# Cutting the first two chunks' products at two quarters and a half of the weights, in an attention and MoE kernel

## The chip, the core and the metric

The kernel runs on one core of a Trainium2 chip. The metric is device time in microseconds (us) of one execution. Engines are named as the profile names them: PE (matrix products), PEld (its weight loads), DVE (vector), ACT (scalar), POOL (GpSimd), SP (the engine whose queue issues the transfers).

## The reference

Attention with four sink keys and a sliding window of 128 keys, over 4 batches, 8 heads, 768 positions and 64 channels, feeds a two-layer feed-forward block:

```python
scores = scale * np.matmul(q, k.transpose(0, 1, 3, 2))
keep = is_sink | in_window
scores = np.where(keep, scores, -1000000000.0)
a = np.exp(scores - np.max(scores, axis=-1, keepdims=True))
x = np.matmul(a / (np.sum(a, axis=-1, keepdims=True) + 1e-09), v)   # regrouped to 3072 tokens x 512
h = np.maximum(x @ w_in, 0.0)                                       # w_in 512 x 2048
return (h * h @ w_out).astype(np.float32)                           # w_out 2048 x 512
```

The inputs are float64. `w_in` and `w_out` therefore arrive as 64-bit words.

## The kernel before, in words

**Chunks and pairs.** The 3072 tokens are cut into 8 chunks of 384 (`NCHUNK`, `TOK`), two to a batch. The attention of a chunk goes by 4 pairs of heads. For one pair: `score` (L240) multiplies queries and keys into a bank of PSUM, tile `s`; DVE adds the mask and takes the row's extreme (L268, `P` and `nbs`); ACT takes the exponential (L271); `normalise` (L275) takes reciprocals on DVE (`rs`) and scales on POOL (L296), which also gathers the sink columns in `PSK` (L302, L303); `probs` (L337) transposes on PE into tile `pt` and ACT or DVE copies it out as `PTF` (L357, L355); `sink_keys` (L305) does the same for the sinks (`pss`, `SK`); `values` (L383) multiplies into `xo`, and ACT and DVE write the chunk's `x` in a high and a low part (L409, L410).

**Products.** `moe` (L445) is a generator that works through a list of legs `(c, f0, f1)`: chunk `c` by the slices `f0` to `f1` of the 16 slices of 128 hidden units. One item is one slice of one chunk: 12 multiplications into `ph` (L457), `r` and `gh` on ACT (L465, L468), a second square on ACT (L472) or a product on DVE (L475), the low part `gl` on DVE (L479), and, one item later, 9 multiplications into the three banks `po` (L494). It yields four times an item; one such step is called a quantum here. At a leg's end `evacuate` (L506) empties `po`: of a leg that begins at slice 0 by copies on DVE and ACT (L522, L520), of another by loading the earlier partial sum `part` from DRAM and adding on DVE (L518). What is not the chunk's last leg is written to `part` in DRAM.

**Weight rows.** 32 rows of weights (`NROW`), 8 to each quarter of the hidden units, are loaded as `raw` (512 KB each, L549) and split into a high and a low part by `split_steps` (L551): on ACT a copy (L560) and a cast (L573), on DVE `t` (L561), `t` again (L563), `m` (L565), `eb` (L567) and the row itself, `wi` or `wo` (L574). It yields in between; a row takes 5 steps. The buffer `m` is single. A row's raw words are loaded two rows ahead.

**Order.** Up to L707 the order on every engine is the one of the code (`manual_schedule`). First comes stage A, five rounds `s` (L653 to L679): scores of pair `s`, values of pair `s-2`, and the transpositions (`tail`) of pair `s-1`, with `fill(n)` putting `n` steps of the split between. Then comes stage B (L699 to L703): in each of `QUANTA` quanta of the first leg, `fill` some steps and one entry of a list `todo`, which holds the attention of pairs 5 to 7 of the first eight (31 entries). Stage B ends when `EARLY` rows are split. After that the legs go on under a scheduler that orders each engine's instructions itself; a table `plan` says up to which unit of later attention and over which rows each leg goes, and `need` (L710) holds rows back no longer than the products allow.

Of the kernel before, what the change touches and what calls it, by code (L numbers as in the profile page):

```python
# [8 lines left out]
F32 = mybir.dt.float32  # L9
# [9 lines left out]
P = 128  # L19
# [22 lines left out]
def sink_window_attention_moe(  # L42
# [25 lines left out]
    with ExitStack() as fast:  # L68
# [437 lines left out]
        def evacuate(c, f0, f1, po):  # L506
            for t in range(NQ):
                pool, tag = (ap3, "PTF") if c == NCHUNK - 1 and t == 2 else (mp, "ob")
                ob = pool.tile([P, DM], F32, tag=tag, name=f"ob_{c}_{f0}_{t}")
# [13 lines left out]
                if f1 < NFC:  # L523
                    part[c, t] = dp.tile([P, DM], F32, tag=f"part{c}{t}", name=f"part_{c}_{t}")
                    nc.sync.dma_start(out=part[c, t], in_=ob)
                else:
                    nc.sync.dma_start(out=out[r0 : r0 + P, :], in_=ob)
# [79 lines left out]

        FH = NFC // 2
        legs = [(0, 0, FH), (1, 0, FH), (0, FH, NFC), (1, FH, NFC)] + [(c, 0, NFC) for c in range(2, NCHUNK)]
        products = moe(legs)  # L610
        QUANTA = 4 * FH
        EARLY = HALF + 2
        with tc.manual_schedule(engines={E.PE, E.DVE, E.Activation, E.Pool, E.SP}):
# [39 lines left out]
            for s in range(NPAIR + 1):  # L653
                if s > 0:
                    load_qk(*pairs[s + 1])
                for i, tags in enumerate((("att", "att"), ("h", "h"), ("o0", "o1"))):
                    scores(s, i, tags)
                    fill(1)
                fill(1)
# [7 lines left out]
                if s > 0:  # L667
                    if s > 1:
                        load_v(*pairs[s])
                    t = tail(s - 1, ("o2", "h"))  # L670
                    next(t)
                    fill(1)
                    if rest:
                        rest()
                    next(t)
                    fill(1)
                    next(t)
                else:
                    fill(1)  # L679
# [19 lines left out]
            for n in range(QUANTA):  # L699
                next(products)  # L700
                fill(2 if n < QUANTA // 2 and n % 3 or n % 4 == 0 or n >= QUANTA - 12 else 1)
                if todo:
# [53 lines left out]

        plan = [(ready[1], EARLY, 27, 1.0), (ready[1] + 24, 27, NROW, 0.7), (ready[2], NROW, NROW, 1.0)]
        plan += [(ready[min(c + 1, NCHUNK - 1)], NROW, NROW, 1.0) for c in range(2, NCHUNK)]
# [221 lines left out]
```

## Time and profile before

| | us |
|---|---|
| median of three runs | 709.92 (709.29 to 710.59) |
| the profiled execution, its own time | 708.76 |
| its span, first to last instruction | 706.7 |
| PE busy | 687.6 (97%) |
| DVE busy | 437.6 (62%) |
| ACT busy | 428.7 (61%) |
| POOL busy | 230.2 (33%) |

The page gives busy time as a share of the whole span. The kernel is not the same all along, though: in the first sixth PE is not always fed, and from there on it nearly always is. What one part of the kernel costs is therefore read from views that are cut by time: the busy time of each engine in a stretch, the instructions of one engine in order of time with the idle time before each and what ended it (in square brackets), and the groups of like instructions in a stretch. In these views a matmul's start is sure and its end modelled, so rows overlap; the time from one start to the next tells more than the duration.

### The profile page before, as it was taken

How to read it: one execution, taken by the hardware profiler on the slowest of the kernel's cores; microseconds unless marked ns; L12 is line 12 of the kernel's file. 1: busy time of each engine (PE TensorE's matmuls, PEld its weight loads, DVE VectorE, ACT ScalarE, POOL GpSimd, SP SyncE). 2: the span in 40 equal slices, each digit the busy share in tenths (PEclk: the TensorE clock that was granted, in tenths of full speed). 3: DMA queues.
4: the chain of work that ended last, by engine and by line, in shares of the span. 5: the costliest groups of instructions: out<-in, count | busy, mean ns of one | idle time of the engine just before them, and what ended most of it. 6: DMA issues, size and time to landing. Idle time of an engine off the chain costs nothing.

```text
span 706.7 us, 11716 instructions
## 1 busy us (share of the span) xinstructions
PE 687.6 (97%) x3866; PEld 593.9 (84%) x3866; DVE 437.6 (62%) x1183; ACT 428.7 (61%) x1200; POOL 230.2 (33%) x436
## 2 busy tenths in 40 slices
PE   8789999999999999999999999999999999999996
PEld 4557788998888888888888888889888898889995
DVE  8998889945657655565656565665555655542231
ACT  5887777755666766766676676667767454422221
POOL 6645400043455424323433443332344233200000
PEclk9999999999999999999999999999999999999998
DMA  8475457421534433333343532344333310000001
GB/s 262 144 233 169 129 163 233 142 74 42 149 65 120 131 107 94 85 108 107 94 112 104 150 90 80 95 128 115 98 88 84 96 44 15 1 11 36 1 0 50
DMA packets 37028, 71.51 MB, mean 101 GB/s; under 512 B 4384, under 2 KB 14368, under 8 KB 36960
## 3 DMA queue, kind: packets, MB, share of 16 engines
q1 hardware_dynamic: 36816, 70.55, 34.1%
q8 instruction: 33, 0.54, 0.3%
q14 instruction: 35, 0.29, 0.1%
q10 hardware_dynamic: 144, 0.13, 0.1%
HBM read 62.80 MB, written 7.86 MB: 100 GB/s over the span
## 4 chain that ended last, share of the span: by engine, by line
PE 86%; ACT 5%; DVE 3%; DMA 3%; issue 1%; SPq 0%; ACTq 0%; DVEq 0%
PE po L494 35%; PE ph L457 35%; PE xo L398 6%; PE s L264 4%; PE pt L368 2%; ACT P L271 2%; PE xo L401 2%; DMA kn<-in_k_dram 1%; PE s L260 1%; PE pt L350 1%; ACT m L560 1%; DVE P L268 1%; DMA part<-ob 1%; PE pss L310 1%; DMA raw<-in_moe_w_in_dram 1%
## 5 line engine op out<-in xcount | busy, mean ns | idle before, releaser
L457 PE MATMUL ph<-x,wi 128*128 128x384 f32 x1536 | 305.8, 340 | 0.0
L457 PEld LDWEIGHTS ph<-x,wi 128*128 128x128 f32 x1536 | 265.0, 188 | 8.8 <-issue 1.4
L494 PE MATMUL po<-wo,gh 128*128 128x512 f32 (+1 forms) x770 | 244.3, 398 | 1.1 <-DVE ob L522 0.6
L232 POOL TENSOR_TENSOR KS<-kn,KS 128x408 fp32r<-128x408 f32 (+1 forms) x48 | 58.5, 1218 | 318.9 <-ACT KS L231 315.1
L494 PEld LDWEIGHTS po<-wo,gh 128*128 128x128 f32 x770 | 135.8, 188 | 19.9 <-issue 1.4
L494 PE MATMUL po<-wo,gl 128*128 128x512 f32 x385 | 151.6, 394 | 0.0
L271 ACT ACTIVATE P<-P,nbs 128x264 f32<-128x264 f32 (+1 forms) x192 | 94.4, 492 | 75.5 <-DVE nbs L268 75.1
L465 ACT ACTIVATE r<-ph 128x384 f32<-128x384 f32 x128 | 62.3, 486 | 91.8 <-PE ph L457 89.2
L475 DVE TENSOR_TENSOR ph<-ph,r 128x384 f32<-128x384 f32 x104 | 58.4, 562 | 72.6 <-ACT r L465 72.5
L268 DVE CUSTOM_DVE_ANT_0 P<-s,masks 128x264 f32<-128x264 f32 x160 | 67.1, 429 | 57.2 <-PE s L264 53.8
L296 POOL TENSOR_SCALAR P<-P,rs 128x136 f32<-128x136 f32 (+2 forms) x192 | 85.4, 460 | 34.6 <-DVE rs L285 17.8
L494 PEld LDWEIGHTS po<-wo,gl 128*128 128x128 f32 x385 | 72.2, 188 | 16.0
L479 DVE TENSOR_TENSOR gl<-ph,gh 128x384 fp32r<-128x384 f32 x128 | 71.1, 556 | 23.3 <-ACT ph L472 12.8
L468 ACT ACTIVATE gh<-r 128x384 fp32r<-128x384 f32 x128 | 67.2, 525 | 3.0
L234 DVE TENSOR_TENSOR QS<-qn,QS 64x384 fp32r<-64x384 f32 x48 | 47.3, 984 | 26.5 <-ACT QS L233 26.1
L291 POOL TENSOR_TENSOR P<-P 128x256 f32<-128x256 f32 (+1 forms) x48 | 50.4, 1050 | 24.1 <-ACT P L271 23.6
L264 PE MATMUL s<-KS,QS 128*128 128x264 f32 (+1 forms) x288 | 57.4, 281 | 0.3 <-DVE nbs L268 0.3
L264 PEld LDWEIGHTS s<-KS,QS 128*128 128x128 f32 x288 | 52.0, 188 | 5.6 <-DVE nbs L268 1.2
L374 DVE TENSOR_TENSOR PTF<-pt,halves 128x256 f32<-128x256 f32 x96 | 36.3, 419 | 22.3 <-PE pt L368 21.7
L398 PE MATMUL xo<-PTF,vn 128*64 128x256 f32 (+1 forms) x448 | 47.4, 348 | 2.5 <-ACT PTF L357 2.5
L398 PEld LDWEIGHTS xo<-PTF,vn 128*64 128x64 f32 x448 | 31.7, 138 | 19.8 <-issue 10.1
L231 ACT CAST KS<-kn 128x408 fp32r<-128x408 f32 (+1 forms) x48 | 28.2, 588 | 32.5 <-issue 18.9
(104 smaller groups left out, 632.4 us busy)
## 6 DMA issues: line engine op xcount, KB each, us to landing
raw<-in_moe_w_in_dram SPq DMA_DIRECT2D x16, 512.0 KB, 4.5
raw<-in_moe_w_out_dram SPq DMA_DIRECT2D x16, 512.0 KB, 3.5
half<-in_moe_w_in_dram SPq DMA_DIRECT2D x32, 256.0 KB, 3.2
half<-in_moe_w_out_dram SPq DMA_DIRECT2D x32, 256.0 KB, 3.0
kn<-in_k_dram SPq DMA_DIRECT2D x24, 272.0 KB, 4.2
qn<-in_q_dram SPq DMA_DIRECT2D x32, 192.0 KB, 3.7
out_dram<-ob SPq DMA_DIRECT2D x23, 256.0 KB, 2.3
kn<-in_k_dram SPq DMA_DIRECT2D x24, 204.0 KB, 3.6
```

Source lines behind the costliest of these rows:

```text
L232: nc.gpsimd.tensor_tensor(KS[:, 1, 0:nk], st["kn"][:, hh, 0:nk], f32(KS[:, 0, 0:nk]), op=ALU.subtract)
L264: nc.tensor.matmul(ps[:, 0:n], st["QS", hh][:, qcols], flat[:, a, c0 : c0 + n], start=(a == 0), stop=(a == 1))
L268: nc.vector.tensor_tensor_reduce(Pt[:, i, 0:n], ps[:, 0:n], mask[:, 0:n], -SCALE, BIG, ALU.add, ALU.min, nb)
L271: nc.scalar.activation(Pt[:, i, 0:n], Pt[:, i, 0:n], AF.Exp, bias=nb, scale=-1.0, accum_out=sm[:, i : i + 1])
L296: nc.gpsimd.tensor_scalar(Pt[:, j, 0:n], Pt[:, j, 0:n], rs[:, hh, j : j + 1], 1.0, op0=ALU.mult, op1=ALU.mult)
L398: nc.tensor.matmul(xo[h * D : h * D + D, cols], lhsT, rhs, start=(n == 0), stop=False, skip_group_check=True)
L457: nc.tensor.matmul(ph[:, 0:TOK], wi_at(i, cc, fc), xt[:, cc, :], start=(m == 0), stop=(m == 3 * NCC - 1),)
L465: nc.scalar.activation(r, ph[:, 0:TOK], AF.Relu)
L468: nc.scalar.activation(gh, r, AF.Square)
L475: nc.vector.tensor_tensor(ph[:, 0:TOK], ph[:, 0:TOK], r, op=ALU.mult)
L479: late = lambda: nc.vector.tensor_tensor(gl, ph[:, 0:TOK], f32(gh), op=ALU.subtract)
L494: nc.tensor.matmul(po[t][:, e], gt[:, ts_], wo[f][:, i, e], start=(f == f0 and j == 0), stop=(f == f1 - 1 and j == 2), skip_group_check=True,)
```

## The change

The first leg pair, chunks 0 and 1 by the first half of the hidden units, becomes two leg pairs, each by a quarter; the second half stays whole. So the legs are (0, first quarter), (1, first quarter), (0, second quarter), (1, second quarter), (0, second half), (1, second half), and then chunks 2 to 7 as before. Stage B lasts 16 quanta in place of 32 and does two entries of `todo` in each, with one or two steps of the split. Rounds 1 to 3 of stage A lose three of their six steps each. `EARLY` falls from 18 rows to 9. The partial sums of the second quarter are loaded, added to and written back, out of the three buffers of `PTF`. The plan for rows and later attention is redrawn: the attention of chunk 2 that lies beside the legs of the second half is 10 and then 59 units where it was 24 and then 45.

```diff
-                pool, tag = (ap3, "PTF") if c == NCHUNK - 1 and t == 2 else (mp, "ob")
+                pool, tag = (ap3, "PTF") if c == NCHUNK - 1 and t == 2 or f0 == NFC // 4 else (mp, "ob")
...
-        FH = NFC // 2
-        legs = [(0, 0, FH), (1, 0, FH), (0, FH, NFC), (1, FH, NFC)] + [(c, 0, NFC) for c in range(2, NCHUNK)]
+        FQ, FH = NFC // 4, NFC // 2
+        cuts = ((0, FQ), (FQ, FH), (FH, NFC))
+        legs = [(c, f0, f1) for f0, f1 in cuts for c in range(2)] + [(c, 0, NFC) for c in range(2, NCHUNK)]
...
-        QUANTA = 4 * FH
-        EARLY = HALF + 2
+        QUANTA = 4 * FQ
+        EARLY = NCC + 5
...
+                ahead = s % NPAIR == 0
                 for i, tags in enumerate((("att", "att"), ("h", "h"), ("o0", "o1"))):
                     scores(s, i, tags)
-                    fill(1)
+                    if ahead or i == NQ - 1:
+                        fill(1)
                 fill(1)
...
-                    fill(1)
+                    if ahead:
+                        fill(1)
                     next(t)
...
-                fill(2 if n < QUANTA // 2 and n % 3 or n % 4 == 0 or n >= QUANTA - 12 else 1)
+                if todo:
+                    todo.pop(0)()
+                fill(1 + n % 2)
                 if todo:
                     todo.pop(0)()
...
-        plan = [(ready[1], EARLY, 27, 1.0), (ready[1] + 24, 27, NROW, 0.7), (ready[2], NROW, NROW, 1.0)]
+        plan = [(ready[1], EARLY, 14, 1.0), (ready[1], 14, 18, 1.0), (ready[1], 18, 23, 1.0)]
+        plan += [(ready[1] + 10, 23, NROW, 0.8), (ready[2], NROW, NROW, 1.0)]
```

On ACT, between rounds 1 and 2 of stage A (the tiles `P_1`, `PTF_0` and `P_2` are those of pairs 1, 0 and 2), the kernel before has:

```order
L271 ACTIVATE P_1_1_255,sm_1_249<-P_1_1_255,nbs 128x264
L357 COPY PTF_0_0_313<-pt_0_0_308 128x512
L573 CAST wi<-t_1_260 128x512
L560 COPY m_340<-raw_177 128x512
L357 COPY PTF_0_2_349<-pt_0_2_344 128x512
L271 ACTIVATE P_2_0_357,sm_2_356<-P_2_0_357,nbs 128x128
```

and the changed kernel:

```order
L271 ACTIVATE P_1_1_255,sm_1_249<-P_1_1_255,nbs 128x264
L561 COPY m_277<-raw_171 128x512
L357 COPY PTF_0_0_311<-pt_0_0_306 128x512
L357 COPY PTF_0_2_339<-pt_0_2_334 128x512
L271 ACTIVATE P_2_0_347,sm_2_346<-P_2_0_347,nbs 128x128
```

The two instructions of the split that stood between the two `PTF` copies are gone from there; one of the row before stands ahead of them.

On PE, at the first transpositions of stage B (`pt_0` and `pss_0` are pair 0 of chunk 1), the kernel before has:

```order
L350 MATMUL pt_0_0_746<-ident,P_0_0_545 128x128 x4
L457 MATMUL ph_1_733<-x_0_411,wi 128x384 x2
L457 MATMUL ph_1_733<-x_0_412,wi 128x384
L457 MATMUL ph_1_733<-x_0_411,wi 128x384 x2
L457 MATMUL ph_1_733<-x_0_412,wi 128x384
L310 MATMUL pss_0_770<-ident,PSK_145 128x128 x2
L350 MATMUL pt_0_1_775<-ident,P_0_0_545 128x128
```

and the changed kernel:

```order
L260 MATMUL s_1_0_2_671<-kn_1_517,qn_1_516 128x264
L260 MATMUL s_1_1_2_675<-kn_1_517,qn_1_516 128x264
L350 MATMUL pt_0_0_699<-ident,P_0_0_522 128x128 x4
L310 MATMUL pss_0_711<-ident,PSK_145 128x128 x2
L350 MATMUL pt_0_1_716<-ident,P_0_0_522 128x128
L350 MATMUL pt_0_1_716<-ident,P_0_1_527 128x128
L350 MATMUL pt_0_1_716<-ident,P_0_0_522 128x128
L350 MATMUL pt_0_1_716<-ident,P_0_1_527 128x128
L350 MATMUL pt_0_2_724<-ident,P_0_1_527 128x128 x4
L457 MATMUL ph_1_735<-x_0_399,wi 128x384 x2
```

The products that stood between the first transposition and the next ones now stand behind all of them.

On DVE, after 16 items, between the `gl` of the last item of one leg and that of the first item of the next but one, the kernel before has:

```order
L479 TENSOR_TENSOR gl_7_1661<-ph_7_1645,gh_7_1660 128x384
...
L567 TENSOR_SCALAR eb_1885<-t_30_1883 128x512
L522 COPY ob_0_0_1746<-po_0_0_1399 128x512
L574 SCALAR_TENSOR_TENSOR wo_1891<-m_1884,eb_1885 128x512
L268 ISA P_0_0_1736,nbs<-s_0_0_0_1737,mask_117 128x128
L268 ISA nbs 128x1
L479 TENSOR_TENSOR gl_8_1726<-ph_8_1686,gh_8_1725 128x384
```

and the changed kernel:

```order
L479 TENSOR_TENSOR gl_7_1645<-ph_7_1629,gh_7_1644 128x384
...
L575 SCALAR_TENSOR_TENSOR wi<-m_1803,eb_1804 128x512
L564 SCALAR_TENSOR_TENSOR t_27_1839<-raw_1775,t_27_1839 128x512
L519 TENSOR_TENSOR ob_4_0_1736<-po_4_0_1561,ob_4_0_1736 128x512
L519 TENSOR_TENSOR ob_4_1_1741<-po_4_1_1562,ob_4_1_1741 128x512
L479 TENSOR_TENSOR gl_8_1704<-ph_8_1671,gh_8_1703 128x384
L519 TENSOR_TENSOR ob_4_2_1746<-po_4_2_1563,ob_4_2_1746 128x512
```

Copies out of `po` (of which ACT takes one in three) are now three adds on DVE, and the split stands at row 27 where it stood at row 30.

## Rows read from the trace of the kernel before

**Rows 1.** From the page: busy us of the engines, share of the span, instructions.

```profile
PE 687.6 (97%) x3866; PEld 593.9 (84%) x3866; DVE 437.6 (62%) x1183; ACT 428.7 (61%) x1200; POOL 230.2 (33%) x436
```

**Rows 2.** Busy time by stretch (stage B, five items of the second leg, and the fourth leg): PE, PEld, DVE, ACT, POOL with the number of instructions, then PE's granted clock, the share of the DMA engines and GB/s.

```profile
41.08:97.24 56.16, 54.12 (x321) 41.49 (x321) 47.97 (x121) 44.84 (x106) 23.67 (x36) 1.00 0.52 164
...
112.75:133.44 20.69, 20.69 (x105) 18.77 (x105) 20.69 (x47) 16.85 (x32) 0.00 (x0) 1.00 0.53 170
...
178.20:225.00 46.80, 46.07 (x271) 39.74 (x270) 30.11 (x95) 30.59 (x88) 22.94 (x43) 1.00 0.44 113
```

**Rows 3.** PE in order of time, the scores of rounds 2 and 4, the values of pair 3, and the first product: start, us, instruction, and in brackets the idle time before it and what ended it.

```profile
18.93 1.38 PE L260 MATMUL s<-kn,qn 64*128 64x128 f32 x10 [1.30 <-ACT PTF L357]
...
31.60 2.21 PE L260 MATMUL s<-kn,qn 64*128 64x264 f32 x12 [1.76 <-ACT PTF L357]
...
39.04 1.88 PE L398 MATMUL xo<-PTF,vn 128*64 128x256 f32 x12 [2.48 <-ACT PTF L357]
...
41.08 1.21 PE L457 MATMUL ph<-x,wi 128*128 128x384 f32 x6
```

**Rows 4.** ACT in order of time in stage A, at the end of rounds 1 and 3 (columns as in rows 3).

```profile
17.67 0.77 ACT L560 COPY m<-raw 128x512 uint16<-128x512 uint16 x1 [1.42 <-issue]
...
29.46 0.60 ACT L573 CAST wi<-t 128x512 fp32r<-128x512 f32 x1
29.97 0.76 ACT L560 COPY m<-raw 128x512 uint16<-128x512 uint16 x1
30.60 0.46 ACT L409 CAST x<-xo 128x384 fp32r<-128x384 f32 x1
```

**Rows 5.** DVE in order of time in the second leg: one row of the split runs from one L561 to the next, with a `gl` further on.

```profile
119.28 0.42 DVE L561 TENSOR_SCALAR t<-raw 128x512 int32<-128x512 int32 x1
...
121.50 0.43 DVE L561 TENSOR_SCALAR t<-raw 128x512 int32<-128x512 int32 x1
...
123.04 0.56 DVE L479 TENSOR_TENSOR gl<-ph,gh 128x384 fp32r<-128x384 f32 x1
123.50 0.46 DVE L565 TENSOR_SCALAR m<-raw 128x512 uint16<-128x512 uint16 x1
```

**Rows 6.** The end of POOL's work on pair 2, and the PE transposition that follows it.

```profile
28.21 0.22 POOL L303 TENSOR_TENSOR PSK<-P,PSK 128x16 fp32r<-128x16 f32 x1
...
28.92 0.27 PE L310 MATMUL pss<-ident,PSK 128*128 128x128 f32 x1
```

**Rows 7.** Units of PE's work. From the chain of waits, the 9 `po` and 12 `ph` of an item (start, us); then from PE in order of time, where the next row's start gives a unit's length: a pair of scores, the sinks' and a transposition, the values of a pair.

```profile
112.75 2.08 PE po L494 x9
114.83 2.08 PE ph L457 x12
...
42.21 0.72 PE L260 MATMUL s<-kn,qn 64*128 64x264 f32 x4
42.86 1.31 PE L457 MATMUL ph<-x,wi 128*128 128x384 f32 x6
...
81.76 0.38 PE L310 MATMUL pss<-ident,PSK 128*128 128x128 f32 x2
81.98 0.60 PE L350 MATMUL pt<-ident,P 128*128 128x128 f32 x4
82.33 1.29 PE L457 MATMUL ph<-x,wi 128*128 128x384 f32 x6
...
77.47 1.57 PE L398 MATMUL xo<-PTF,vn 128*64 128x256 f32 x16
...
79.25 0.62 PE L494 MATMUL po<-wo,gh 128*128 128x512 f32 x2
```

**Rows 8.** The two longest waits of PE in stage B (41.08 to 97.24 us): total, times, longest.

```profile
PE pt L350 <- ACT PTF L357: 0.8, 1, 0.8
PE s L260 <- DVE nbs L268: 0.8, 1, 0.8
```

**Rows 9.** Groups of ACT in stage B: count, busy us and mean ns of one, idle time before them.

```profile
L560 ACT COPY m<-raw 128x512 uint16<-128x512 uint16 x12 | 9.3, 777 | 0.8 <-DVE wo L574 0.4 <-DVE wi L574 0.4
L271 ACT ACTIVATE P<-P,nbs 128x264 f32<-128x264 f32 x18 | 9.1, 507 | 3.2 <-DVE nbs L268 3.2
...
L573 ACT CAST wo<-t 128x512 fp32r<-128x512 f32 x7 | 4.3, 612 | 0.0
L468 ACT ACTIVATE gh<-r 128x384 fp32r<-128x384 f32 x8 | 4.2, 524 | 0.2
L465 ACT ACTIVATE r<-ph 128x384 f32<-128x384 f32 x8 | 3.9, 482 | 1.5 <-PE ph L457 1.5
```

**Rows 10.** Waits at the ends of legs: PE and DVE after the first leg, PE after the third.

```profile
110.03 0.73 PE L494 MATMUL po<-wo,gh 128*128 128x512 f32 x2 [0.63 <-DVE ob L522]
...
109.28 0.69 DVE L522 COPY ob<-po 128x512 f32<-128x512 f32 x1 [1.11 <-DMA part<-ob]
...
182.85 0.73 PE L494 MATMUL po<-wo,gh 128*128 128x512 f32 x2 [0.47 <-DVE ob L518]
```

**Rows 11.** A stretch of stage A (columns as in rows 2), and twice the same values, from PE in order of time.

```profile
21.00:22.00 1.00, 1.00 (x8) 0.62 (x5) 1.00 (x6) 1.00 (x4) 0.63 (x2) 0.50 0.00 0
...
20.24 2.27 PE L398 MATMUL xo<-PTF,vn 128*64 128x256 f32 x12
...
27.03 1.30 PE L398 MATMUL xo<-PTF,vn 128*64 128x256 f32 x12
```

More of the change, by code (lines that the diff above doesn't have):

```diff
@@ L523, in evacuate @@
                 if f1 < NFC:
-                    part[c, t] = dp.tile([P, DM], F32, tag=f"part{c}{t}", name=f"part_{c}_{t}")
+                    part[c, t] = dp.tile([P, DM], F32, tag=f"part{c}{t}", name=f"part_{c}_{f0}_{t}")
                     nc.sync.dma_start(out=part[c, t], in_=ob)
```

## The prediction

> **What bounds the kernel now.** I read the page first: PE is busy for 687.6 of 706.7 us [rows 1], so nothing but PE's own work and the few stretches in which it is not fed can count. Then I read busy time by stretch. From 112.75 us on, five items of products take 20.69 us without a gap [rows 2], 4.14 each: one set of 12 `ph` is 2.08 us from start to start, one of 9 `po` as much [rows 7]. From there to the end PE has work in hand, so the end of the kernel is the moment at which PE is fed for good, plus a fixed amount of work. The change takes no product away. What it can win lies ahead of that moment, in stage A and stage B.
>
> Stage A ends at 41.08 us with the first `ph` [rows 3]. In it PE waits for ACT's `PTF` copies before each round's scores, 1.30 us in round 2 and 1.76 in round 4, and 2.48 before the last values [rows 3]. Stage B lasts from 41.08 to 97.24 us, where PE has done 8 sets of `ph`, 7 of `po` and the attention of chunk 1. Its busy share there is 54.12 of 56.16 us [rows 2], but a matmul's end is modelled, so I count the work itself. A pair of scores takes 42.86 - 42.21 = 0.65 us, a transposition group 82.33 - 81.98 = 0.35, the sinks' 81.98 - 81.76 = 0.22, the values 79.25 - 77.47 = 1.78 [rows 7]. Nine scores, 12 transpositions, 4 sinks and 4 values make 5.85 + 4.2 + 0.9 + 7.1 = 18.0; with 15 x 2.08 = 31.2 that is 49.2. So stage B loses 7.0 us, of which only some 2 show as idle; 1.6 are the two longest waits [rows 8].
>
> The Trainium skill, Perfetto Trace Analysis, section Identifying the Most-Contended Engine, says that the busy share of matmuls is no good measure of how near PE is to its limit. By the share taken at its word stage B would have 2.0 us to give, by the count 7.0; the sum below goes by the count.
>
> **The change part by part.**
>
> *Stage A, nine split steps fewer.* A row of the split takes 121.50 - 119.28 = 2.22 us of DVE for five steps [rows 5], so nine steps are 9/5 x 2.22 = 4.0 us of DVE, and on ACT two copies and two casts. PE's waits there are on ACT, so I follow ACT. At the end of round 1 the second `PTF` copy stands behind a copy `m` that sat idle for 1.42 us until 17.67 and then held ACT to 18.31, where the copy could start [rows 4]; without it the copy can follow its transposition, about 17.2: 1.1 us. In round 2 two steps no longer lie between DVE's score reductions; ACT's exponentials follow at most partly: 0.5. At the end of round 3 a cast and a copy leave ACT, from 29.46 to 30.60 [rows 4]: 1.1. What is late next is POOL: it ended pair 2 at 28.43 and PE's `pss` followed at 28.92 [rows 6]; pair 2 begins 1.6 earlier by then, so POOL allows 2.7 in all with little to spare. In round 4 the same number of steps stays, one of them out of the scores' way: 0.4. Sum 3.1, products from 38.0 us. Bounds: 1.1 if only the first holds, 4.0 if DVE sets the pace.
>
> *Stage B in 16 quanta.* PE's work is 4 `ph`, 3 `po` and the same attention: 7 x 2.08 + 18.0 = 32.6 us. DVE loses 7 rows (15.5 us) and 4 items from its 47.97 and is no bound. ACT is: its 44.84 us [rows 2] lose four items (half of 4.2, and as much again for the squares' `r`) and 7 rows at 0.777 + 0.612 us [rows 9], 13.8 in durations, some 11.6 since neighbours overlap by about 0.1: 33.2. ACT and PE are then equally full, and the banks pass from one to the other. At the first transpositions nothing lies between the three any more. Two banks serve them; the second bank is the sinks', so the next transposition needs ACT's first `PTF` copy. ACT has six exponentials (0.6 each), two squares (0.5 each) and a cast (0.6) ahead of it, and the scores feed it from 1.9 us after the start of the stage: that copy ends near 7.4 (with 0.58 for itself), while PE is there after 2.1 + 1.95 + 0.35 + 0.22, with the changes between kinds of work some 5.0. PE waits 2.4, and 0.7 more for the sinks' copies: 3.1. The 1.6 of waits before go into this; of the other 5.4 lost before I keep two thirds, 3.6, since half the products go and all attention stays. Stage B: 32.6 + 3.1 + 3.6 = 39.3 us, to 77.3.
>
> At that point PE is four items behind the kernel before at 97.24; level with it stands 97.24 - 4 x 4.14 = 80.7. So 3.4 us are gained, 3.1 of them in stage A. Bounds for stage B: 36 (the waits alone gone) and 43.8, where ACT's 33.2 would keep all its idle time of before, 56.16 - 44.84 = 11.3, less 0.7 for items gone.
>
> *More ends of legs.* Six in place of four. Before, two of the four cost PE time: 0.63 and 0.47 us [rows 10]. Two more at 0.5, with three adds each on DVE: +0.7 (0 to 1.5). The loads wait for nothing PE does, and three buffers take them at once.
>
> *DVE in the legs of the quarters.* The rows taken out ahead come back here. From the last `gl` of stage B's leg to that of slice 11 the new order has 16 items, in 66.2 us of PE, and on DVE 22.6 rows x 2.22 + 16 `gl` x 0.46 [rows 5] + 10 copies and adds x 0.6 (0.69 less the overlap with the next) [rows 10] + 2 of attention = 65.5. That is full. In the five items of rows 2 DVE was full too, 20.69 of 20.69, and PE lost nothing; the third multiplication of a `po` comes some 3 us after its `gl` could be made, so a short lag is hidden. DVE's wait for a `part` buffer, 1.11 us [rows 10], comes twice now. I take +0.5 (0 to 3).
>
> *Chunk 2's attention, 59 units beside eight items where it was 45.* The fourth leg ran at 30 of 46.8 us on DVE and ACT [rows 2]; the 14 units more add under a third to either and 4 to 5 us of PE work beside it. No new wait: 0 (0 to 1.5). These units come out of the third leg, so their work is no extra.
>
> Sum: -3.4 + 0.7 + 0.5 = -2.2 us. The profiled execution took 708.76 (span 706.7 and 2.06 around it), so it would be 706.6; it lay 1.16 under the median of 709.92, so the median becomes 707.7.
>
> **The rivals.**
>
> *The pace of stage A was DVE's throughout, and stage B is fed better* (few rows left in it): 4.0 and 36 us, level point 73.1, so -7.6 + 1.2 = -6.4, 703.5. For it: nine steps leave DVE and only two instructions of each kind ACT. Against: each listed wait of PE there is on ACT.
>
> *ACT starves PE in stage B*, the slower side. Place: transpositions and values of chunk 1, packed twice as densely; price: stage B at 43.8 in place of 39.3, level point 81.8, so +1.1 + 1.2 = +2.3, 712.2. It decides from a stage B longer than 80.7 - 38.0 = 42.7 us, less what the legs cost. For it: the order on PE and 33.2 us of ACT in about 39. Against: ACT's longest idle before was waiting for PE and DVE, which now come sooner.
>
> *DVE cannot make up the rows*: products of the fourth quarter, or `gl`, come late by the 3 us above. Then -3.4 + 0.7 + 3.0 = +0.3, about 710. It speaks for it that no slack is left in 66 us, against it the five items with DVE at 100% and PE unharmed.
>
> *The clock.* Near 21 us PE's granted clock is 0.50 of full, 1.2 GHz [rows 11], after a stretch with the 1.30 us idle of rows 3; a set of values takes 2.27 us there and 1.30 at full clock [rows 11]. A fall of that kind inside stage B would cost near 1.7 us of products: -0.5, 709.4. The waits of 1.76 and 2.48 us in rows 3 brought no fall, which speaks against it. The Trainium skill, TensorE: Matmul & The Clock Gate, section A second HAM failure mode: psum-queue depth-cycling, warns that short idle spells between groups that rotate through banks can make the clock swing; by that rule the packed transpositions of stage B would be the place, and no run here shows it yet.
>
> **How the numbers follow.** Forecast 0.46, between 705.8 and 709.4; the earlier stage A at DVE's pace 0.14; ACT starving PE 0.18; DVE short of time 0.15; the clock 0.07. About 0.2% (1.4 us) is what a measurement of this kernel tells from no change, so faster means under 708.5 and slower over 711.3. Faster: four fifths of the forecast, 0.37, all of the second case, 0.14, and little else: 0.53. Slower: most of the starved case and a tail of the short DVE, 0.18. Same: 0.29. The range runs from 703.0 to 712.2, the two outer cases.
>
> **What would show it.** `ph` of the first item near 38.0 us, with the wait before round 2's scores gone; the third leg's `ph` (chunk 0, slice 4) near 77.3 + 17; PE's waits on `PTF` in the first 10 us of stage B near 3 us; DVE at 95% or more from there for 65 us, with PE's waits on `ob` near 2 us. A first product later than 40, or a stage B over 43, would make the forecast wrong, and so would PE idle on `wi` or `gl` around slice 12.

## The result, and the profile after

The changed kernel takes 716.11 us (median of 4, 715.29 to 716.48) where the kernel before, on the same chip, takes 709.61 (709.29 to 710.59): a ratio of 1.0085, interval 1.0073 to 1.0098. It is slower by 6.5 us. The forecast of 707.7 and its range up to 712.2 were wrong. The profiled execution of the changed kernel took 716.48 us (span 714.8).

The page of the changed kernel, busy time and the clock in 40 slices; the first line answers to [rows 1]:

```profile
PE 690.2 (97%) x3865; PEld 596.2 (83%) x3866; DVE 435.3 (61%) x1185; ACT 429.9 (60%) x1204; POOL 223.0 (31%) x436
...
PEclk9989999999999999999999999999999999999998
```

The shares are those of before, and say nothing. The third slice of the clock (35.7 to 53.6 us) shows 8, where the kernel before shows 9 in every slice but the last; most of it lies in stage B. PE in order of time at the end of stage A (columns as in [rows 3]):

```profile
17.83 1.38 PE L260 MATMUL s<-kn,qn 64*128 64x128 f32 x10 [0.26 <-ACT PTF L357]
...
28.17 2.46 PE L260 MATMUL s<-kn,qn 64*128 64x264 f32 x12 [0.23 <-ACT PTF L357]
...
35.96 1.82 PE L398 MATMUL xo<-PTF,vn 128*64 128x256 f32 x12 [2.58 <-ACT PTF L357]
...
38.08 2.13 PE L457 MATMUL ph<-x,wi 128*128 128x384 f32 x6
```

The waits of 1.30 and 1.76 us in [rows 3] are 0.26 and 0.23 now, the one of 2.48 is 2.58, and the first product stands at 38.08. Three stretches of the changed kernel, columns as in [rows 2]: stage B, the 16 items behind it, and items 12 to 34 (chunk 1's second quarter to chunk 2's third item):

```profile
38.08:83.40 45.32, 40.70 (x239) 30.09 (x239) 27.46 (x80) 32.10 (x82) 18.75 (x37) 0.93 0.42 134
83.40:149.60 66.20, 63.57 (x320) 57.00 (x320) 61.70 (x135) 48.67 (x93) 0.00 (x0) 1.00 0.69 231
119.57:235.44 115.87, 113.07 (x634) 98.87 (x632) 83.01 (x228) 75.07 (x196) 39.99 (x74) 1.00 0.42 128
```

PE is busy for 40.70 of 45.32 us in stage B, at a mean granted clock of 0.93. Its waits there (total, times, longest) answer to [rows 8]:

```profile
PE s L260 <- DVE nbs L268: 1.8, 3, 0.6
PE pt L350 <- ACT PTF L357: 1.6, 2, 1.2
PE pt L350 <- DVE nbs L268: 0.6, 1, 0.6
PE pt L350 <- ACT SK L317: 0.3, 1, 0.3
```

PE and DVE at the ends of the first, second and fifth leg, then a wait of PE in chunk 2's second item and the DVE instruction that held up the reduction it waited for; the first five answer to [rows 10]:

```profile
95.32 0.73 PE L494 MATMUL po<-wo,gh 128*128 128x512 f32 x2 [1.33 <-DVE ob L523]
...
110.89 0.73 PE L494 MATMUL po<-wo,gh 128*128 128x512 f32 x2 [1.30 <-DVE ob L523]
...
184.53 0.73 PE L494 MATMUL po<-wo,gh 128*128 128x512 f32 x2 [1.22 <-DVE ob L519]
...
94.57 0.69 DVE L523 COPY ob<-po 128x512 f32<-128x512 f32 x1 [1.72 <-DMA part<-ob]
...
110.14 0.69 DVE L523 COPY ob<-po 128x512 f32<-128x512 f32 x1 [1.47 <-DMA part<-ob]
...
226.11 0.51 PE L264 MATMUL s<-KS,QS 128*128 128x264 f32 x2 [1.13 <-DVE nbs L268]
...
223.99 1.59 DVE L234 TENSOR_TENSOR QS<-qn,QS 64x384 fp32r<-64x384 f32 x1 [0.36 <-ACT QS L233]
```

Count the items from 0 in order of time. From item 12 on (chunk 1's fifth slice) both kernels do the same items in the same order, so the first `ph` of an item can be set side by side. Items 0, 12, 16 and 34 start at 41.08, 114.67, 131.36 and 227.99 us before, at 38.08, 119.57, 136.26 and 235.44 after. The changed kernel is 3.0 us ahead, then 4.9 behind, and 7.45 behind at item 34, where it stays (last product 699.37 and 706.74). At the end of stage B, 83.40, a quarter of a fifth `ph` is done, so four `ph` and three `po` stand at 82.9, which is 2.2 behind 80.7, the moment at which the kernel before is as far (97.24 less four items). That splits the loss: stage B turns -3.0 into +2.2; the first two legs' ends add 2.7; the legs with chunk 2's attention add 2.55. The other 0.7 us of the spans lies behind the last product (8.0 us against 7.3, from its start), a time that lies anywhere from 6.3 to 8.6 us in the runs below. The executions profiled lie 7.7 us apart, the medians 6.5: that of the changed kernel is the slowest of its four.

### The profile page after: what moved, and what is told of

Its sections match the earlier page's. It is cut to its first block, busy times and chain, and to the rows that moved or that the text cites. A ratio compares the mean times of both kernels' runs of the same rounds, so it can differ in the third digit from the quotient of the medians.

```text
span 714.8 us, 11772 instructions
## 1 busy us (share of the span) xinstructions
PE 690.2 (97%) x3865; PEld 596.2 (83%) x3866; DVE 435.3 (61%) x1185; ACT 429.9 (60%) x1204; POOL 223.0 (31%) x436
## 4 chain that ended last, share of the span: by engine, by line
PE 87%; ACT 4%; DVE 3%; DMA 3%; issue 1%; POOL 1%; SPq 0%; DVEq 0%; ACTq 0%; POOLq 0%
PE ph L457 35%; PE po L494 35%; PE xo L398 6%; PE s L264 4%; PE pt L368 2%; ACT P L271 2%; PE xo L401 2%; DMA part<-ob 1%; PE s L260 1%; PE pt L350 1%; POOL P L296 1%; PE pss L310 1%; DMA out_dram<-ob 1%; DVE P L268 1%; DMA raw<-in_moe_w_in_dram 1%
## 5 line engine op out<-in xcount | busy, mean ns | idle before, releaser
L475 DVE TENSOR_TENSOR ph<-ph,r 128x384 f32<-128x384 f32 x100 | 56.2, 562 | 72.4 <-ACT r L465 72.1
L296 POOL TENSOR_SCALAR P<-P,rs 128x136 f32<-128x136 f32 (+2 forms) x192 | 81.4, 440 | 32.4 <-DVE rs L285 18.7
L398 PE MATMUL xo<-PTF,vn 128*64 128x256 f32 x448 | 46.4, 343 | 2.6 <-ACT PTF L357 2.6
```

The costliest lines, as they stand in the source:

```text
L296: nc.gpsimd.tensor_scalar(Pt[:, j, 0:n], Pt[:, j, 0:n], rs[:, hh, j : j + 1], 1.0, op0=ALU.mult, op1=ALU.mult)
L398: nc.tensor.matmul(xo[h * D : h * D + D, cols], lhsT, rhs, start=(n == 0), stop=False, skip_group_check=True)
L475: nc.vector.tensor_tensor(ph[:, 0:TOK], ph[:, 0:TOK], r, op=ALU.mult)
```

## The experiments

One table for all, then run by run. "Stage B" runs from the first `ph` to the end of chunk 1's last values; "4 to 12" and "12 to 34" are times between first `ph`s of items, from PE in order of time; "falls" are stretches of the profiled execution between 34 and 60 us at a clock of 0.50 (1.2 GHz). Ratios are to runs of the kernel before on the same chip. Stage B of the kernels by halves holds four items more, and "4 to 12" of these begins inside it.

| kernel | us | ratio (interval) | first `ph` | stage B | falls | 4 to 12 | 12 to 34 |
|---|---|---|---|---|---|---|---|
| before | 709.6 | 1 | 41.08 | 55.5 | 0 | 46.2 | 113.3 |
| after | 716.1 | 1.0085 (1.0073, 1.0098) | 38.08 | 45.3 | 2 | 40.11 | 115.9 |
| e1_light_a | 708.4 | 0.9976 (0.9965, 0.9987) | 38.76 | 57.2 | 0 | 45.9 | 113.3 |
| e2_warm | 716.8 | 1.0094 (1.0077, 1.0111) | 40.08 | 43.0 | 0 | 39.2 | 118.0 |
| e3_evac3 | 711.7 | 1.0025 (1.0011, 1.0038) | 38.62 | 43.9 | 1 | 37.08 | 115.5 |
| e4_banks | 713.9 | 1.0061 (1.0041, 1.0080) | 37.81 | 41.8 | 1 | 38.5 | 115.9 |
| e5_plan24 | 711.4 | 1.0018 (1.0004, 1.0032) | 38.05 | 45.5 | 2 | 37.06 | 113.5 |
| e6_all | 707.4 | 0.9969 (0.9958, 0.9979) | 38.84 | 42.0 | 2 | 37.07 | 112.8 |
| e7_halves | 706.8 | 0.9959 (0.9946, 0.9972) | 37.54 | 57.2 | 0 | 45.6 | 113.7 |
| e8_rows_early | 715.9 | 1.0089 (1.0074, 1.0104) | 40.97 | 43.9 | 0 | 36.9 | 115.6 |
| e9_two | 708.8 | 0.9982 (0.9970, 0.9995) | 37.70 | 41.9 | 1 | 37.09 | 115.7 |
| e10_halves_all | 710.7 | 1.0004 (0.9993, 1.0014) | 38.72 | 61.5 | 2 | 45.8 | 113.8 |
| e11_third | 711.7 | 1.0015 (1.0003, 1.0026) | 39.38 | 61.9 | 2 | 45.7 | 113.4 |
| e12_quarters_all | 708.6 | 0.9979 (0.9966, 0.9992) | 38.56 | 41.3 | 1 | 37.10 | 114.0 |
| e13_sink_back | 707.6 | 0.9961 (0.9946, 0.9976) | 38.48 | 57.5 | 1 | 45.6 | 113.7 |
| e14_plan_alone | 712.8 | 1.0039 (1.0024, 1.0055) | 37.75 | 43.1 | 0 | 38.8 | 113.3 |
| e15_fill | 707.1 | 0.9951 (0.9933, 0.9969) | 37.89 | 40.3 | 0 | 37.06 | 113.5 |
| e16_plan10 | 709.7 | 0.9988 (0.9978, 0.9998) | 38.76 | 57.3 | 0 | 45.7 | 115.3 |

**e1_light_a: stage A's part alone, in the kernel before.**

```diff
+                ahead = s % NPAIR == 0
-                    fill(1)
+                    if ahead or i == NQ - 1:
+                        fill(1)
...
-        EARLY = HALF + 2
+        EARLY = HALF
```

(the `if ahead` ahead of the tail's second `fill` too; stage B's `fill` makes up the steps)

> The kernel before with one part of the change alone: nine split steps fewer in rounds 1 to 3 of stage A (legs of half the weights, 32 quanta, and 16 rows where it had 18 by the end of stage B; the nine steps are made up in stage B, which keeps its number of steps). Theory: stage A's gain is real and carries through, so the first product stands near 38.1 us and the median falls by the whole 3.0 us, to some 706.6. Rival: the rows put off take the gain back in stage B or the second leg (two rows more there, 4.4 us of DVE), and the time is 709 to 710.

Faster, by 0.24%, about 1.7 us; between the two theories. The trace shows the first product 2.3 us earlier, not 3.0, and one cause is a `pss` that came late from POOL.

```profile
16.38 0.33 PE L310 MATMUL pss<-ident,PSK 128*128 128x128 f32 x1 [1.14 <-POOL PSK L303]
```

The kernel before has no such wait in its execution, the changed kernel one of 0.30 and e6_all, with the same order there, one of 1.15, so it differs between executions. Of the 2.3, 1.3 are left at item 12; that the rows put off took the 1.0 back, as the rival has it, fits and is not shown. Stage A's part is a gain.

**e2_warm: PE kept at work.**

```diff
+            busy(8)
             rest = values(*pairs[NPAIR - 1], True)
...
                 sink_keys(*a, spare[0])
+                if s == NPAIR:
+                    busy(5)
...
+                if n in (0, 1):
+                    busy(2)
                 fill(1 + n % 2)
```

> The changed kernel with products of constants (they compute nothing that is used) in PE's idle spots: 8 before the last values of stage A, 2 and 2 among the first scores of stage B, 5 ahead of its second transpositions. Theory of the clock: the two falls to 0.50 at 37.5 and 47.7 us follow idle spells and cost some 3.4 us of stage B; with the spells filled they do not come, stage B is 41.5 to 42 us and the median 712.5 to 713. Rival, waits alone: the same copies are waited for, the filler takes time of its own, and the median is 716 to 717.

No fall came between 34 and 60 us, and stage B is 2.3 us shorter than after's. But the filler wrote to bank `o2` and had to wait itself, so the first product is 2.0 us later:

```profile
36.80 1.90 PE L632 MATMUL idle<-idle 128*128 128x512 bf16 x7 [2.43 <-DVE SK L317]
```

Its items 12 to 34 also took 118.0 us, with a wait of 2.03 for an `ob` and a fall of the clock at 186 us, where no other profiled execution has one. The median is the rival's, but with these losses in it it decides nothing; the clock's theory needed a better filler (e15_fill).

**e3_evac3: three buffers at the first two legs' ends.**

```diff
-or f0 == NFC // 4 else (mp, "ob")
+or c < 2 and f0 < NFC // 2 else (mp, "ob")
```

> The changed kernel with the partial sums of the first two legs copied out through the three buffers of PTF in place of the two of ob. Theory: PE's waits of 1.33 and 1.30 us at the ends of these legs are for the third copy, which waits for a buffer whose transfer to DRAM stands behind weight loads; with three buffers they fall to 0.5 or less each, and the median by 1.6 to 2.0 us, to 714.3. Rival: DVE is the bound over these legs, and what is saved is waited for later: 716.

0.60% less than after, more than expected. From 83.40 on PE has no gap, and items 4 to 12 take 37.08 us in place of 40.11; every later kernel with this edit and quarters takes 37.1, e8_rows_early 36.9.

```profile
83.40:115.66 32.26, 32.26 (x162) 28.90 (x161) 31.77 (x69) 25.11 (x48) 0.00 (x0) 1.00 0.73 239
```

So the ends cost 3.0 us in after's execution. In those of e2_warm, e4_banks and e14_plan_alone, which keep two buffers, items 4 to 12 take 38.5 to 39.2: 1.4 to 2.1 us. DVE at 31.77 of 32.26 does not matter: the rival falls. In the traces the last product comes 4.2 us earlier than after's; 3.0 of that lie here and 1.4 in stage B, where this execution has one fall of the clock less.

**e4_banks: free banks for stage B's first scores.** `scores` takes its tags from a table; the first tail's sinks use `o0`, its last transposition `o1`.

```diff
+                    tags = {(5, 1): ("o0", "o1"), (5, 2): ("o2", "xo"), (6, 1): ("o0", "o1")}
...
-                t = tail(s - 1, ("att", "att"))
+                t = tail(s - 1, ("o0", "att", "o1") if s == NPAIR + 1 else ("att", "att", "att"))
```

> The changed kernel with the first scores and transpositions of stage B spread over banks that are free until the first po (o0, o1, o2, xo) in place of two banks alone. Theory of the waits: PE's waits of 0.64, 0.62, 1.19 and 0.64 us between 41 and 53 us are for banks; 2.5 to 3.1 us of stage B go, and if the second clock fall goes with them, 2 more: median 711 to 713.5. Rival: the chain from scores over DVE and ACT to PTF has the same length whatever banks it uses, PE waits for it one step later, and the median is 715.5 to 716.5.

0.24% less than after, between the two theories. PE's waits in its stage B (total, times, longest):

```profile
PE s L260 <- ACT PTF L357: 1.7, 2, 1.1
PE s L260 <- DVE nbs L268: 0.5, 1, 0.5
PE pt L350 <- ACT PTF L357: 0.5, 1, 0.5
```

Both theories have a share: the waits for DVE and at the transpositions shrink from 4.3 us to 1.3, and 1.7 us at the next scores, which wait for the same `PTF` copies, are new. From the start of pair 3's transpositions (near 32 us in both) to the end of stage B, e6_all with these banks and two falls takes 49.0 us, after 51.4: the banks are worth 2.4 in these two executions.

**e5_plan24, e14_plan_alone, e9_two, e16_plan10: the units beside chunk 0's and chunk 1's last legs.** One number is changed: in e3_evac3 and in the changed kernel as shown; e9_two is e6_all without it; e16_plan10 turns the 24 of e7_halves into 10:

```diff
-(ready[1] + 10, 23, NROW, 0.8)
+(ready[1] + 24, 23, NROW, 0.8)
```

> e3_evac3 (the changed kernel, first two legs copied out through three buffers, 711.67) with one number of the plan as it was before: 24 units of chunk 2's attention beside chunk 0's last leg and 45 beside chunk 1's, in place of 10 and 59. Theory of the density: the last two legs of the changed kernel end 2.2 to 2.5 us later than before's (item 12 to item 34: +0.99 to +3.18 us in e3_evac3), because 59 units beside eight items leave PE waiting for DVE; with 24 and 45 the median falls by 1.7 to 2.5 us, to 709.2 to 710. Rival: the loss is the work of the same units at another place, and the median stays at 711 to 712.

> e6_all (707.40) without its third part: three buffers and free banks, but the units of chunk 2 at 10 and 59 as in the changed kernel. It repeats the question that e5_plan24 left open, where the last two legs were 2.0 us shorter in the trace and the median only 0.2 lower. Theory of the density: from item 12 to item 34 this kernel takes 115.2 to 116 us where e6_all takes 112.8, and the median is 709 to 710. Rival: the plan is worth nothing and the median is 707 to 708.

> The changed kernel (716.1) with 24 and 45 units in place of 10 and 59, and nothing else. Theory of the density: items 12 to 34 take 113 to 114 us in place of 115.87, and the median is 713.6 to 714.6. Rival: the plan is worth nothing in the median, 715.3 to 716.5.

> e7_halves (706.83) with the changed kernel's numbers for chunk 2's attention: 10 and 59 units in place of 24 and 45. Theory of the density: items 12 to 34 get 2 to 2.5 us longer and the median is 708.6 to 709.4. Rival: only where the attention stands is changed and not the time, 706.5 to 707.3.

The traces speak with one voice: items 12 to 34 take 115.3 to 115.9 us with 10 and 59 units and 112.8 to 114.0 with 24 and 45 (e2_warm's 118.0 aside). The medians are less plain. In the changed kernel alone (e14_plan_alone) the number is worth 0.46%, and put the other way into e7_halves (e16_plan10) it costs 0.29%: both are clear of the noise. e6_all against e9_two gives 0.13% and e5_plan24 against e3_evac3 0.07%, both within it, and e5_plan24's median lies where the rival had it. All four have the same sign.

The mean granted clock, which is on record for every run, explains a part. In e3_evac3 and e5_plan24 it goes with the time: 709.9 to 710.2 us at 0.997 and 712.9 to 713.4 at 0.990 in the first, 709.7 at 0.998 and 713.1 to 713.4 at 0.990 in the second. With one straight line of time against clock for each pair (an estimate), e6_all is 1.6 us under e9_two at like clock, and e5_plan24 0.6 under e3_evac3. PE's waits between items 12 and 34, in e7_halves:

```profile
PE po L494 <- DVE ob L518: 1.2, 1, 1.2
PE pt L368 <- DVE PTF L377: 0.3, 1, 0.3
```

and in e16_plan10:

```profile
PE s L264 <- DVE nbs L268: 1.1, 1, 1.1
PE po L494 <- DVE ob L518: 0.6, 1, 0.6
```

The wait of 1.1 us for DVE before a score is there in all kernels with 59 units beside that leg. Of those with 45, e11_third and e12_quarters_all, which put one more partial sum into `PTF`, show 0.8, the kernel before 0.3, the others none. The wait for an `ob` comes with either number (none to 1.5 us with 45, 0.6 to 2.0 with 59). The other part is PE's busy time, 0.9 us more on the same work; why is open, and e12_quarters_all, with 45, has as much (113.1). The stretch in e7_halves, then in e16_plan10:

```profile
111.82:225.53 113.71, 112.19 (x633) 99.12 (x632) 79.38 (x217) 74.97 (x195) 39.91 (x74) 1.00 0.39 110
```

```profile
113.10:228.42 115.32, 113.12 (x634) 98.95 (x633) 77.39 (x217) 74.28 (x195) 39.98 (x74) 1.00 0.37 109
```

So after against before loses 2.55 us in this stretch, and the one number is worth 2.5 of them in e14_plan_alone and 1.6 to 2.9 in the other pairs.

**e6_all: all three.** The edits of e3_evac3, e4_banks and e5_plan24 together.

> The changed kernel with all three: three buffers at the first two legs' ends, the free banks at the start of stage B (e4_banks), and 24 and 45 units. If the three losses are separate they add up: 716.1 less 4.4, 2.3 and 2.0 is 707.4, between 706.5 and 708.5. Rival: they overlap, as PE waits once for what any of them delays, and the sum is 709 or more.

707.40, as forecast. By ratios, after less what e3_evac3, e4_banks and e14_plan_alone gave is 0.9955; measured is 0.9969, with that inside the noise of the four (some 0.4%). The losses add up as far as that shows; an overlap of a third of them would not.

**e8_rows_early: stage A's steps as before,** in e3_evac3.

```diff
-                    if ahead or i == NQ - 1:
-                        fill(1)
+                    fill(1)
...
-                    if ahead:
-                        fill(1)
+                    fill(1)
```

> e3_evac3 with the split steps of stage A as they were before (nine more in rounds 1 to 3, so nine fewer, 1.8 rows, in stage B). Theory that stage B is a chain of scores, DVE, ACT, PTF with too little PE work beside it: its length, 43 to 44.5 us, does not fall by more than 1 us, the first product comes near 41, and the median is 713 to 714.5. Rival, ACT and DVE are loaded down by rows of the split in stage B: 1.8 rows are 2.5 us of ACT and 4 of DVE, stage B falls to 40 to 41.5, and the median is 710.5 to 712.

Slower than e3_evac3, by 0.64%, and above what either theory gave. In the traces the last product is 2.3 us later, and the first one 2.35; why the medians are 4.5 us apart is open. The premise held only half: with the first nine rows ready early, the scheduler drew the rows of the next legs into the end of stage B.

```profile
40.97:84.87 43.90, 38.28 (x240) 27.86 (x240) 35.86 (x99) 37.05 (x91) 20.94 (x36) 1.00 0.53 166
```

ACT and DVE are 5 and 8 us busier than in after's stage B, and yet it is but 0.8 us longer than in e14_plan_alone (43.08, also without a fall), as much as a wait for `PTF` ahead of the seventh values that is new. Up to the end of the fifth values, where there really were fewer rows, it took 17.9 us against 18.5. How full ACT is hardly sets the length of stage B.

**e7_halves: stage A's part and three buffers, legs by halves,** from e1_light_a.

```diff
-if c == NCHUNK - 1 and t == 2 else (mp, "ob")
+if c == NCHUNK - 1 and t == 2 or c < 2 and f0 == 0 else (mp, "ob")
```

> e1_light_a (the kernel before with the lighter stage A, 708.38) with three buffers at the ends of the first two legs, which here are halves. The kernel before waited 0.63 us at the first of these ends; e1_light_a shows no such wait over 0.3. So the theory of the ends gives 0.2 to 0.6 us at most: 707.8 to 708.4. Rival: the three copies in a row also free DVE and the queue sooner, as in e3_evac3 where the two ends gave 3 us: 706.5 to 707.5.

706.83, the lowest median in us: 0.41% under before, 1.3% under after (by ratio e15_fill is as low). That is in the rival's range, but the step from e1_light_a is 0.17%, within the noise, and in the trace only 0.3 us of it lie between items 4 and 12, as the theory had it; 1.2 us more come in stage A, which the edit does not touch.

**e10_halves_all, e11_third, e12_quarters_all: two more edits.** e10_halves_all puts free banks into e7_halves and moves a split step behind round 4's transpositions:

```diff
+                    tags = {(5, 1): ("o0", "o1"), (5, 2): ("o2", "xo")}
...
-                t = tail(s - 1, ("att", "att"))
+                t = tail(s - 1, ("o0" if s == NPAIR + 1 else "att", "att"))
...
-                    if ahead:
-                        fill(1)
                     next(t)
...
-            fill(2)
+            fill(3)
             rest()
```

e11_third adds the next line, and e12_quarters_all puts its like (`f0 < NFC // 2` for `f0 == 0`) and the moved step into e6_all:

```diff
-or c < 2 and f0 == 0 else
+or c < 2 and (f0 == 0 or t == 2) else
```

> e7_halves (706.83: legs by halves, the lighter stage A, three buffers) with the free banks for the first scores and sinks of stage B, and one split step of round 4 moved behind the transpositions. Theory: PE's waits of 1.2, 0.6 and 0.9 us at 42 to 51 us are for banks and go in part, and 0.5 to 0.6 of the 2.6 us before the last values of stage A goes with the cast that stands between the PTF copies; in all 1.2 to 2.5 us: 704.3 to 705.6. Rival: with products between the scores the chain is hidden already and PE waits for the same copies a step later: 706.3 to 707.

> e10_halves_all with the third partial sum of chunk 0's and chunk 1's last legs loaded into a buffer of PTF in place of a third turn of the two ob. Theory: PE's wait of 1.2 us at the end of chunk 0's last leg (e7_halves) is for an add whose partial sum is loaded only when a buffer is free; it falls to 0.3 or less: 0.5 to 1.0 us less than e10_halves_all. Rival: PTF is then short for chunk 2's attention, which runs beside, and nothing is gained or up to 1 us lost.

> e6_all (707.40: legs by quarters) with the two further edits of e10_halves_all and e11_third, the split step moved and the third partial sum in PTF. If the quarters cost nothing by themselves once their waits are gone, it is level with e11_third, within 0.7 us. Rival: the quarters keep a cost (stage B packed twice as densely, two more leg ends), and it is 1 to 3 us slower than e11_third.

e10_halves_all lost 0.45% against e7_halves, a miss of my own making. PE in order of time:

```profile
51.76 1.22 PE L494 MATMUL po<-wo,gh 128*128 128x512 f32 x2 [4.83 <-ACT SK L317]
```

and the six us in which that wait ends, by busy time and clock:

```profile
50.00:56.00 6.00, 4.24 (x12) 3.46 (x13) 5.34 (x11) 2.46 (x6) 5.15 (x8) 0.53 0.65 193
```

With one entry per quantum the sinks' transposition stands right ahead of the first `po`, which wants the same bank `o0`; ACT empties it late. And from the last part of the 4.8 idle us until 57 us the granted clock is 0.50. e11_third took away the wait of 1.40 for an `ob` and brought one of 0.79 for a score: no gain. e12_quarters_all against e6_all is +0.10%: none either. That e12 beats e11 says nothing of quarters and halves, since e11 has the bad bank.

**e13_sink_back: that one bank put back,** in e10_halves_all.

```diff
-                t = tail(s - 1, ("o0" if s == NPAIR + 1 else "att", "att"))
+                t = tail(s - 1, ("att", "att"))
```

> e10_halves_all (710.67) with the sinks of stage B's first tail back in the bank they had. There PE's first po waited 4.8 us for ACT's copy of the sinks out of bank o0, and the granted clock was 0.50 for 6 us behind it. Theory: that one bank is the whole loss, the wait goes and the time is that of e7_halves (706.8) or up to 2 us less, 704.8 to 707. Rival: the moved split step or the clock did it, and the median stays at 709 or more.

707.6, a little above the forecast, and by ratio, 0.9961, the level of e7_halves: the bank was the whole loss. The free banks for the scores gain nothing here: the wait of 1.2 us at a score is gone and one of 2.4 for `PTF` is there in place of 0.6.

**e15_fill: filler in free banks,** in e6_all.

```diff
-            def busy(n):
+            def busy(n, tag="o2"):
...
+            busy(9, "o0")
             rest = values(*pairs[NPAIR - 1], True)
...
+                if n == 4:
+                    busy(4)
```

> e6_all (707.40) with products of constants (nothing reads them) inside two of PE's waits: 9 ahead of the last values of stage A, in a bank that is free, so that they fit into the wait of 2.6 us, and 4 ahead of the scores that wait 0.7 and 1.1 us in stage B. Theory of the clock: neither fall to 0.50 comes, 1.0 to 1.5 us each as the traces with one fall and with two differ; median 704.8 to 706.4. Rival: the falls come for another reason or cost nothing, and the median is 707 to 708.

PE in order of time at the end of stage A:

```profile
33.39 2.11 PE L631 MATMUL idle<-idle 128*128 128x512 bf16 x8
...
36.13 1.60 PE L398 MATMUL xo<-PTF,vn 128*64 128x256 f32 x12 [0.64 <-ACT PTF L357]
```

The wait of 2.6 is mostly filled. Stage B by busy time, its clock 1.00:

```profile
37.89:78.23 40.34, 37.96 (x243) 28.05 (x243) 27.50 (x81) 31.58 (x82) 19.40 (x37) 1.00 0.49 151
```

No fall, and from 32 us to the end of stage B 46.0 us in place of e6_all's 49.0. The median is 0.18% lower, inside the intervals, and where the rival had it; the profiled execution lost 1.3 us again behind item 34, where PE waited 1.07 for an `ob` at the end of chunk 1's last leg. That the filler is worth 3 us is shown for the stretch, in one execution of either kernel, not for the whole. That it holds the clock the other runs show too: all six have a mean granted clock of 0.996 to 0.998, ten of e6_all's twelve one of 0.990 to 0.994.

## Why the prediction was wrong

**Stage A: right.** 38.0 was forecast, 38.08 came; the wait ahead of round 2's scores gave 1.04 of the 1.1, that ahead of round 4's 1.5. A part is luck: by the starts of the scores, the values and the product, the four terms of 1.1, 0.5, 1.1 and 0.4 came as 1.1, 0.8, 1.5 and -0.4. The clock's fall near 21 us in the kernel before is not behind the gain: e8_rows_early has stage A's steps as before, no fall, and its first product at 40.97. Nine other executions with the same order there lie at 37.5 to 38.8. DVE's pace throughout (the first rival) would have been 37.1: not reached.

**Stage B: the step that failed first.** 39.3 us were forecast, 44.8 measured, by the same count of work; a stage B over 43 had been named as a sign of being wrong. Its terms were 32.6 of work, 3.1 of waits and 3.6 of other loss. The waits measured 1.8 + 1.6 + 0.6 + 0.3 = 4.3: those at the transpositions, 2.5 in all, are near what I had, but I had no term for those between scores, where two entries in one quantum leave nothing to do while DVE empties the two banks: 0.6 us, three times. The clock took 2.2, from after's 45.3 against 43.1 in e14_plan_alone, whose stages A and B are instruction for instruction the same (its profiled execution, 709.03, is the fastest of its seven; the others took 711.9 to 713.7). The remaining 44.8 - 32.6 - 4.3 - 2.2 = 5.7 is the whole of the 5.4 lost before, and in e14_plan_alone, with waits of 4.8, 42.6 - 32.6 - 4.8 = 5.2 remain: "of the other 5.4 I keep two thirds" was wrong. That loss did not shrink with the products; that it goes with the attention fits, but no run shows it. With free banks, filler and no fall (e15_fill) the same work takes 40.3 - 0.5 = 39.8 us, near where I had put it. The third leg's first `ph`, forecast near 94, came at 101.25.

**The rival that came true, and how.** ACT starving PE had the right place, and its end of 43.8 is near the 42.6 of a stage B without falls (43.08 less the quarter of a `ph`). But it is not ACT's load: e8_rows_early put 5 us more on it, for 0.8. It is the chain of scores, DVE, ACT and copy through two banks, which free banks shorten (stage B takes 41.8 us in e4_banks and 43.9 in e3_evac3, with one fall of the clock in each).

**The clock: the rival priced too low.** 0.07, since the waits of 1.76 and 2.48 us had brought no fall. Two windows of 2 us in after, and the same in e14_plan_alone:

```profile
38.00:40.00 2.00, 2.00 (x7) 1.70 (x6) 0.56 (x1) 1.15 (x2) 1.63 (x5) 0.50 0.76 242
48.00:50.00 2.00, 1.85 (x8) 1.48 (x7) 1.55 (x3) 1.37 (x4) 1.85 (x5) 0.50 0.65 246
```

```profile
38.00:40.00 2.00, 1.59 (x10) 0.93 (x8) 0.82 (x2) 1.10 (x2) 1.66 (x5) 1.00 0.62 184
48.00:50.00 2.00, 1.38 (x9) 0.71 (x7) 0.55 (x4) 0.32 (x2) 1.85 (x6) 1.00 0.03 10
```

In one the clock is 0.50 there, behind the wait of 2.58 us and behind three waits of 0.64, 0.62 and 1.19 between 41 and 47.4 us; in the other it is not. My price of 1.7 us for a fall was near: from 32.0 us to the end of stage B it is 51.4 us with two falls, 50.4 with one (e3_evac3) and 48.8 with none (e14_plan_alone), 1.0 and 1.6 each, from one execution of each kind. Its chance, and that there might be two, was the mistake. The Trainium skill, TensorE: Matmul & The Clock Gate, section A second HAM failure mode: psum-queue depth-cycling, puts such swings down to short idle spells between groups that rotate through banks. The place agrees (the clock is 0.50 at 48 us behind three such spells); e14_plan_alone has the same spells and no fall, so here they make a fall possible and not certain.

**Ends of legs: mis-sized.** "Two more at 0.5: +0.7" measured 2.7 to item 12, and 3.0 went with three buffers in place of two (1.4 to 2.1 in the other executions with two). I priced an end by the 0.63 of [rows 10], which was one wait of DVE for a `part` transfer, 1.11 us; now it came twice, at 1.72 and 1.47. A transfer to or from `part` lands after 4.1 us in the median, 3.0 in the kernel before; I put that down to the weight loads beside it (DMA share 0.69 over 83.40:149.60, 0.53 in [rows 2]), which no run takes away. I had seen that the wait comes twice, and put it under DVE's pace at +0.5 for all.

**DVE full: nothing, not +0.5.** DVE is busy for 61.7 of 66.2 us in after. In e6_all it is fuller, and PE has no gap:

```profile
83.40:149.60 66.20, 66.20 (x337) 59.84 (x336) 65.42 (x145) 51.50 (x104) 5.45 (x7) 1.00 0.69 231
```

**Chunk 2's attention: the step "No new wait: 0 (0 to 1.5)" failed.** It measured 2.55. I had added up busy time over the leg (a third more of 30 in 46.8 us) and found room; the loss is in single waits, one of 1.13 us behind DVE's `QS` (1.59 us long) that stands ahead of the score's reduction (0.3 before), one of 1.22 for a partial sum (0.47 before), and 0.8 more of PE's busy time, whose cause is open.

**The sum.** -3.4 to the end of stage B was +2.2, +1.2 was +2.7, 0 was +2.55: -2.2 against +7.4 at the last product.

## What to carry to other kernels

When two stages are packed more densely, count the links of the chain (score, reduction, exponential, copy) and the banks between them, not the busy shares: half of the products left stage B here, and its loss stayed. A leg's end needs as many buffers as it has copies where the writes land late, as they do here (4.1 us). And a change made of several parts is best taken apart: stage A's part with three buffers at the legs' ends, and legs by halves as before, takes 706.8 us where before takes 709.6 to 710.3 and the changed kernel 716.1.

## What the runs showed of the hardware

- The clock's falls are not settled by the program: with the same instructions in stages A and B, after and e5_plan24 show two between 34 and 60 us, e3_evac3 one, e14_plan_alone none. The kernel before, e1_light_a, e7_halves and e16_plan10 wait 2.5 to 2.6 us at the end of stage A as well and show none there. Why was not settled. With products of constants in the idle spots neither of two executions fell between 34 and 60 us (e2_warm, e15_fill), and e15_fill's six runs have mean granted clocks of 0.996 to 0.998 where e6_all's twelve have 0.990 to 0.997.
- The runs of one kernel differ with the clock: e3_evac3 takes 709.9 to 710.2 us at a mean granted clock of 0.997 and 712.9 to 713.4 at 0.990.
- From issue to landing, a transfer to or from `part` took 2.3 to 5.9 us in after (median 4.1), for 256 KB, and 2.0 to 4.9 in before; these lines are of after and of before:

```profile
DMA to landing us min/median/max: 2.3/4.1/5.9
DMA to landing us min/median/max: 2.0/3.0/4.9
```

- A bank lent to another use for one copy made PE wait 4.8 us at once, and the granted clock was 0.50 from the last part of that wait until 57 us (e10_halves_all).
